# A fused retention, expert and channel-mix kernel: another spread of the weight-narrowing steps and another order inside the last routing step

## The chip, the cores and the metric

One core of one Trainium2 chip runs the whole program in one launch. The metric is the device time in microseconds (us) of that core, median of the runs; lower is better. Engine names in the rows: PE is the matrix engine (TensorE), PEld its weight loads, DVE VectorE, ACT ScalarE, POOL GpSimd, SP SyncE, which here only issues transfers.

## The reference

Three layers, one after the other, over 2 sequences of 768 tokens with 512 channels:

```python
# 1. retention over 8 heads of 64 channels, in blocks with a decayed state
intra = (q @ k^T * Dmask) @ v ;  inter = (q * lam_pow) @ kv_state ;  x = intra + inter
# 2. eight experts, one per token; a token may keep the expert of the token before it
logits = x @ w_gate ; local = sigmoid(x @ w_local)
e[s] = argmax(logits[s]) if s == 0 or local[s] < 0.5 else e[s-1]
x[s] = softmax(logits[s])[e] * (relu(x[s] @ w1[e]) @ w2[e])          # w1 512x1024, w2 1024x512
# 3. channel mix
xk = mu_k*x + (1-mu_k)*x_prev ;  xr = mu_r*x + (1-mu_r)*x_prev
out = sigmoid(xr @ w_r) * (relu(xk @ w_k)**2 @ w_v)
```

The inputs `w_k`, `w_v` and `w_r` are 64-bit floats; the kernel reads their words and turns them into 32-bit numbers itself.

## The kernel before, in words

**Split products.** Each product of two matrices runs as three (`split3`, L652): each factor is a high part, made by a cast on ACT, and a low part, made by a subtraction on DVE. For the expert weights this is `w_split` (L144): one piece of 128x1024 numbers (512 KB) is cast on ACT (L155, `w1h` or `w2h`), subtracted on DVE (L156, `w1l` or `w2l`), and then the next piece's load is queued on SP (`w_load`, L136). Four pieces (`raw`, pool `stp`) can be staged; a load waits until DVE has read the piece that had its buffer.

**First stage, to about 80 us.** Retention over 12 tiles of 128 tokens (u = 0 to 11). Then the tokens are routed, two tiles at a time, by `route` (L476), a generator whose parts are woven between the tiles' work by `step()`. The last routing (tiles 10 and 11) has nothing behind it to hide under: `logits` (L346) of both tiles, a transpose and a running maximum (`sc`), the expert of each token and its one-hot row (`ohs`, L497), counts of tokens per expert on PE (L500 to L510, into `pr` and `tot`), and from these the permutation `perm` (L516) that puts the last tiles' rows into expert 0's block. The other rows of expert 0 are gathered early (`early_rows`, L382) and transposed on PE (`first_inputs`, L435); the last rows are added to the same accumulators through `perm` (`last_inputs`, L449), with their high and low parts `xlh` and `xll`. Then a branch on the largest count (`overflow`, L388) follows, and the slots of all tokens (`slot`).

**Expert stage, about 80 to 286 us.** For e = 0 to 7: `up` (L659, four blocks `ps_h` of 24 products; ACT makes `hh`, DVE makes `hl` of each block; three accumulators, so the fourth block of `up` waits until the first block's `hh` and `hl` have been made), `flip` (L642, transposes of the next expert's gathered rows), `down` (L699, `ps_y`, two halves). After each block of `up` and twice in each half of `down`, the function `side_w` (L932) is called: 8 calls c per expert, 64 in all. A call splits one weight piece (more in the first calls) and advances the narrowing of the channel-mix weights by `ns` steps. All engines work through their instructions in the order of the program text, so what a call puts on ACT or DVE stands ahead of the next block's `hh` and `hl`.

**Narrowing** (`narrow`, L754) turns 64-bit words into 32-bit numbers, 20 parts of 128x512. A part is three steps on DVE: `narrow_1` (L743, L744), `narrow_2` (L747, L748), `narrow_3` (L751, L752). At the end of a part's third step, ACT takes the magnitudes of the next part (`begin`, L739, tile `t1`), the read of the part after the next is queued on SP (L767, 512 KB into one of two buffers `raw64`), and in the following call the finished part is written to memory (L788, 256 KB, tile `t2`). 61 steps in all; which call does how many stands in `side_w`. In expert 1 a block `weights` (L807) of small DVE and ACT work follows `flip`.

**Last stage, to the end.** The channel mix in six groups of 256 tokens, with the narrowed weights split like the experts' (the last 9 of 73 pieces).

## Time and profile before

| | us |
|---|---|
| time before, median of 3 runs | 474.19 |
| the 3 runs | 473.14 to 475.46 |
| the profiled execution's own time | 471.66 |
| its span (first to last instruction) | 470.0 |
| PE busy | 441.2 (94%) |
| DVE busy | 311.1 (66%) |
| ACT busy | 229.2 (49%) |

The profile is one execution. A row of a timeline gives start, length, engine, line, operation, output<-input, and in brackets the time that the engine stood idle before it and who released it. A row of a table of stretches gives, for each engine, its busy time in the stretch, then the granted clock of PE (1.00 is 2.4 GHz, 0.50 is 1.2 GHz), the busy share of the transfer engines and their rate. Durations of PE overlap with the next product's; the distance between starts is what counts.

### The profile page before, as it was taken

Reading aid. Unit: us, or ns where it says so; the run is one execution under the profiler, and the core shown is the slowest. Engines: PE = TensorE matmul, PEld = TensorE weight load, DVE = VectorE, ACT = ScalarE, POOL = GpSimd, SP = SyncE. Lnnn points to the kernel's source line nnn. Section 1 sums busy time; section 2 is a strip of 40 time slices with the busy share of each in tenths; the row PEclk is TensorE's granted clock in tenths of the full one; section 3 lists DMA queues with packets and bytes.
Section 4 is the critical chain, followed back from the end, with each engine's and each line's share of the span. In section 5 each row is a group of like instructions: output and inputs, shape, how many; then the busy total and the mean of one; then the engine's idle time right before and its main releaser. Section 6 shows DMA issues by size and latency. Waiting matters only on the chain.

```text
span 470.0 us, 8309 instructions
## 1 busy us (share of the span) xinstructions
PE 441.2 (94%) x3243; PEld 394.1 (84%) x3243; DVE 311.1 (66%) x602; ACT 229.2 (49%) x386; POOL 67.2 (14%) x92
## 2 busy tenths in 40 slices
PE   7999988997595799999999999999999999999996
PEld 6878876977585689898989899989898998989886
DVE  6578775767887898999998775655436253361501
ACT  2455523553663456565656463676446264563410
POOL 3432223501201103142300200100000000000000
PEclk9999999999799799999999999999999999999999
DMA  7899944697768889999988640300202002000011
GB/s 240 301 377 326 376 180 135 215 329 250 248 246 276 262 267 339 306 342 354 355 296 300 209 155 22 113 2 1 91 1 67 24 0 91 0 24 23 1 45 46
DMA packets 29111, 85.03 MB, mean 181 GB/s; under 512 B 4351, under 2 KB 5131, under 8 KB 29068
## 3 DMA queue, kind: packets, MB, share of 16 engines
q1 hardware_dynamic: 25004, 73.45, 46.2%
q0 software_dynamic: 2624, 8.39, 4.9%
q10 hardware_dynamic: 1440, 2.62, 1.5%
q8 instruction: 26, 0.43, 0.3%
q14 instruction: 17, 0.14, 0.1%
HBM read 68.71 MB, written 15.74 MB: 180 GB/s over the span
## 4 chain that ended last, share of the span: by engine, by line
PE 62%; DVE 8%; DMA 7%; ACT 4%; issue 1%; SPq 0%; DVEq 0%; ACTq 0%
PE ps_y L657 5%; PE ps_y L655 5%; PE ps_y L656 5%; PE ps_v L655 5%; PE ps_v L656 5%; PE ps_v L657 5%; PE ps_h L655 5%; PE ps_h L656 4%; PE ps_h L657 4%; PE ps_k L1028 4%; PE ps_k L1029 4%; PE ps_k L1035 4%; DMA raw<-in_wk_dram 3%; DMA wk<-t 3%; PE ps_r L656 2%; PE ps_r L655 2%
## 5 line engine op out<-in xcount | busy, mean ns | idle before, releaser
L655 PE MATMUL ps_h<-xsTh,w1h 128*128 128x256 f32 x256 | 74.4, 291 | 16.4 <-DVE hl L670 16.4
L656 PE MATMUL ps_h<-xsTl,w1h 128*128 128x256 f32 x256 | 74.0, 289 | 0.1
L657 PE MATMUL ps_h<-xsTh,w1l 128*128 128x256 f32 x256 | 73.6, 287 | 0.0
L655 PEld LDWEIGHTS ps_h<-xsTh,w1h 128*128 128x128 f32 x256 | 50.3, 197 | 17.6 <-DVE hl L670 16.8
L1067 DVE TENSOR_TENSOR sq<-rl 128x512 f32<-128x512 f32 x24 | 16.6, 691 | 55.9 <-ACT rl L1064 55.9
L655 PE MATMUL ps_y<-w2h,hh 128*128 128x512 f32 (+1 forms) x136 | 52.6, 387 | 0.0
L657 PE MATMUL ps_y<-w2h,hl 128*128 128x512 f32 (+1 forms) x136 | 52.1, 383 | 0.0
L656 PE MATMUL ps_y<-w2l,hh 128*128 128x512 f32 (+1 forms) x136 | 51.9, 382 | 0.0
L656 PEld LDWEIGHTS ps_h<-xsTl,w1h 128*128 128x128 f32 x256 | 50.3, 197 | 0.9 <-DVE xsTl L174 0.5
L657 PEld LDWEIGHTS ps_h<-xsTh,w1l 128*128 128x128 f32 x256 | 50.2, 196 | 0.0
L156 DVE TENSOR_TENSOR w1l<-raw,w1h 128x1024 fp32r<-128x1024 f32 x38 | 46.0, 1216 | 6.3 <-ACT w1h L155 6.3
L156 DVE TENSOR_TENSOR w2l<-raw,w2h 128x1024 fp32r<-128x1024 f32 x35 | 42.7, 1220 | 5.8 <-ACT w2h L155 5.2
L155 ACT CAST w1h<-raw 128x1024 fp32r<-128x1024 f32 x38 | 38.9, 1052 | 4.9 <-DMA raw<-in_w_dram 4.9
L726 POOL DMA_INDIRECT Y_n<-y,sidx x16 | 18.5, 1157 | 153.2 <-ACT y L716 108.4
L655 PE MATMUL ps_v<-w2h,k2h 128*128 128x512 f32 (+1 forms) x104 | 39.2, 377 | 0.0
L656 PE MATMUL ps_v<-w2l,k2h 128*128 128x512 f32 (+1 forms) x104 | 38.8, 373 | 0.0
L657 PE MATMUL ps_v<-w2h,k2l 128*128 128x512 f32 (+1 forms) x104 | 38.8, 373 | 0.0
L155 ACT CAST w2h<-raw 128x1024 fp32r<-128x1024 f32 x35 | 36.6, 1045 | 3.7 <-DMA raw<-in_w_dram 3.7
L739 ACT ACTIVATE t<-raw 128x512 f32<-128x512 f32 x20 | 13.5, 673 | 48.7 <-DMA raw<-in_wk_dram 24.8
L669 ACT ACTIVATE hh<-ps_h 128x512 fp32r<-128x512 f32 x32 | 19.1, 596 | 24.9 <-PE ps_h L657 24.9
L657 PEld LDWEIGHTS ps_y<-w2h,hl 128*128 128x128 f32 x136 | 25.6, 188 | 6.1 <-DVE hl L670 0.8
L656 PEld LDWEIGHTS ps_y<-w2l,hh 128*128 128x128 f32 x136 | 25.6, 188 | 5.1
(210 smaller groups left out, 975.7 us busy)
## 6 DMA issues: line engine op xcount, KB each, us to landing
raw<-in_w_dram SPq DMA_DIRECT2D x64, 512.0 KB
kv<-in_kv_dram SPq DMA_DIRECT2D x12, 512.0 KB
qk<-in_qk_dram SPq DMA_DIRECT2D x11, 512.0 KB
raw<-in_wk_dram SPq DMA_DIRECT2D x8, 512.0 KB
raw<-in_wv_dram SPq DMA_DIRECT2D x8, 512.0 KB
out_dram<-o SPq DMA_DIRECT2D x11, 256.0 KB
X_n<-xn ACTq DMA_DIRECT2D x10, 256.0 KB
xg<-Y_n SPq DMA_DIRECT2D x10, 256.0 KB
```

The source lines that it names most:

```text
L155: act.copy(out=hi[:, j : j + m, :], in_=t)
L156: eng.tensor_tensor(out=lo[:, j : j + m, :], in0=t, in1=hi[:, j : j + m, :].bitcast(F32), op=ALU.subtract)
L655: pe.matmul(ps, wh, xh, start=first, stop=False)
L656: pe.matmul(ps, wh, xl, start=False, stop=False)
L657: pe.matmul(ps, wl, xh, start=False, stop=last)
L669: act.activation(out=hh, in_=ps, func=AF.Relu)
L726: pool.indirect_dma_start(out=Y_n[:, :], out_offset=bass.IndirectOffsetOnAxis(ap=sidx[:, t, e : e + 1], axis=0), in_=y, in_offset=None)
L739: act.activation(out=t.bitcast(F32), in_=words(raw)[2], func=AF.Abs)
L1028: pe.matmul(ps[:, j, :], wkh[:, d, f], x[0][:, d, :], start=j == d == 0, stop=False, skip_group_check=True)
L1029: pe.matmul(ps[:, j, :], wkl[:, d, f], x[0][:, d, :], start=False, stop=False, skip_group_check=True)
L1035: pe.matmul(ps[:, j, :], wkh[:, d, f], x[1][:, d, :], start=False, stop=d == ND - 1, skip_group_check=True)
L1067: dve.tensor_tensor(out=sq, in0=rl, in1=rl, op=ALU.mult)
```

## The change

Five edits:

1. The steps per call (`side_w`). Before: call 2 does one step, calls 4 to 23 do 30 (two in ten of them), calls 24 to 51 one each, call 52 two. After: call 2 does one, calls 4 to 51 one each, and two where c % 8 == 5; calls 52, 53 and 54 do two each. 61 steps in both.
2. The tile `t2` gets three buffers in place of two.
3. In the last routing, the transposes `first_inputs` move from before the counts on PE to behind them; the four idle products (`warm(4)`) that stood there go, and three such products (`warm(3)`) stand where the transposes were.
4. One weight split moves from before `values` of the last tile to behind it, ahead of `logits` of tile 11.
5. The low part of tile 10's rows (`xll`, first half) is made on DVE beside that of tile 11, in place of POOL.

```diff
--- before.py
+++ after.py
@@ -374,7 +374,6 @@
             act.copy(out=hi[:, 0, :], in_=pt[:, 0])
             act.copy(out=xn[NU - B], in_=pt[:, 0])
             act.copy(out=hi[:, 1, :], in_=pt[:, 1])
-            pool.tensor_tensor(out=lo[:, 0, :], in0=xn[NU - B], in1=hi[:, 0, :].bitcast(F32), op=ALU.subtract)
             act.copy(out=xn[NU - 1], in_=pt[:, 1])
             for u in range(NU - B, NU):
                 sp.dma_start(out=X_n[1 + u * P : 1 + (u + 1) * P, :], in_=xn[u])
@@ -508,7 +507,8 @@
                 pe.matmul(tot, ones, acc, start=True, stop=False)
                 for b in range(B):
                     pe.matmul(tot, ones, oh[:, b, :], start=False, stop=b == B - 1)
-                warm(4, "pk")
+                first_inputs(0)
+                first_inputs(1)
                 oh0 = ap.tile([P, B], F32, name="oh0", bufs=1)
                 dve.tensor_copy(oh0, oh[:, :, 0])
                 perm = ap.tile([P, B, CAP], F32R, name="perm0", tag="kd", bufs=1)
@@ -518,7 +518,8 @@
                     )
                 late["perm"] = perm
                 hi, lo = late["x"]
-                dve.tensor_tensor(out=lo[:, 1, :], in0=late["nat"][:, 1], in1=hi[:, 1, :].bitcast(F32), op=ALU.subtract)
+                for b in range(B):
+                    dve.tensor_tensor(out=lo[:, b, :], in0=late["nat"][:, b], in1=hi[:, b, :].bitcast(F32), op=ALU.subtract)
                 for x in (hi, lo):
                     last_inputs(x, (0, 1))
                 for b in range(B):
@@ -606,8 +607,8 @@
                 load_kv(i + 3)
             if i == NU:
                 early_rows()
+                values(i - 1, {1: lambda: logits(i - 2)})
                 w_split()
-                values(i - 1, {1: lambda: logits(i - 2)})
                 logits(i - 1)
                 routing.append(route((i - 2) // B))
         step()
@@ -616,8 +617,7 @@
         step()
         warm(3, "pk")
         step()
-        first_inputs(0)
-        first_inputs(1)
+        warm(3, "pk")
         step()
         step()
         w_split()
@@ -776,7 +776,7 @@
             yield
             begin(0)
             for k in range(len(parts)):
-                t2 = tp.tile([P, n], I32, name="t2", tag="t2")
+                t2 = tp.tile([P, n], I32, name="t2", tag="t2", bufs=3)
                 narrow_1(ts[k])
                 yield
                 narrow_2(raws[k], ts[k], t2, ts[k])
@@ -888,7 +888,7 @@
 
         def mix_pair(i, a, hi, lo, old, new, quick=False):
 
-            t, m = (tp.tile([P, 2, 2 * P], F32, name=x, tag=x) for x in ("t1", "t2"))
+            t, m = (tp.tile([P, 2, 2 * P], F32, name=x, tag=x, bufs=k) for x, k in (("t1", 2), ("t2", 3)))
             r = slice(2 * a, 2 * a + 2)
 
             def older(j):
@@ -937,10 +937,10 @@
             ws, ns, vs = 1, 1, 0
             if c < 4:
                 ws, ns = (2, 2, 1, 1)[c], c == 2
-            elif c < 24:
-                ns = 2 if c % 8 in (4, 6) or c in (5, 7, 13, 15) else 1
             elif c >= 52:
-                ws, ns, vs = ((1, 2, 0), (1, 0, 0), (1, 0, 0), (1, 0, 0), (1, 0, 0), (1, 0, 1), (1, 0, 0), (0, 0, 1), (1, 0, 0), (1, 0, 0), (0, 0, 0), (0, 0, 0))[c - 52]
+                ws, ns, vs = ((1, 2, 0), (1, 2, 0), (1, 2, 0), (1, 0, 0), (1, 0, 0), (1, 0, 1), (1, 0, 0), (0, 0, 1), (1, 0, 0), (1, 0, 0), (0, 0, 0), (0, 0, 0))[c - 52]
+            elif c % 8 == 5:
+                ns = 2
             w_split(ws)
             for _ in range(ns):
                 next(conv, None)
```

ACT around calls 5 to 8 (the second half of expert 0's `down` and the first block of expert 1's `up`); `t<-raw` is the magnitude of a narrowing part (L739), raw_0, raw_1, raw_2 being the parts' reads, `y` a finished half of `down`, `hh` the first block of `up`. Before:

```order
L155 CAST w1h_1566<-raw_1462 128x1024
L739 ACTIVATE t_1597<-raw_1_1499 128x512
L716 COPY y_0_1604<-ps_y_0_1553 128x512
L155 CAST w1h_1566<-raw_1495 128x1024
L739 ACTIVATE t_1628<-raw_2_1599 128x512
L155 CAST w1h_1566<-raw_1532 128x1024
L716 COPY y_1_1655<-ps_y_1_1606 128x512
L669 ACTIVATE hh_0_1682<-ps_h_0_1657 128x512
L155 CAST w2h_1686<-raw_1570 128x1024
```

After:

```order
L155 CAST w1h_1565<-raw_1461 128x1024
L739 ACTIVATE t_1596<-raw_1_1498 128x512
L716 COPY y_0_1600<-ps_y_0_1552 128x512
L155 CAST w1h_1565<-raw_1494 128x1024
L155 CAST w1h_1565<-raw_1531 128x1024
L716 COPY y_1_1642<-ps_y_1_1602 128x512
L669 ACTIVATE hh_0_1669<-ps_h_0_1644 128x512
L155 CAST w2h_1673<-raw_1569 128x1024
L739 ACTIVATE t_1681<-raw_2_1598 128x512
```

The magnitude of the part raw_2 moved from ahead of a weight cast, `y_1` and `hh_0` to behind `hh_0` and one more cast.

DVE up to the first `hl` of expert 1's `up`. Before, from call 5's last instruction (the L744 of the part raw_1) on:

```order
L744 TENSOR_SCALAR t_1597<-t_1597 128x512
L156 TENSOR_TENSOR w1l_1567<-raw_1495,w1h_1566 128x1024
L747 SCALAR_TENSOR_TENSOR t_1601<-raw_1_1499,t_1597 128x512
L748 TENSOR_SCALAR t_1597<-t_1601 128x512
L751 SCALAR_TENSOR_TENSOR t_1597<-raw_1_1499,t_1597 128x512
L752 TENSOR_TENSOR t_1601<-t_1597,t_1601 128x512
L156 TENSOR_TENSOR w1l_1567<-raw_1532,w1h_1566 128x1024
L743 TENSOR_SCALAR t_1628<-t_1628 128x512
L744 TENSOR_SCALAR t_1628<-t_1628 128x512
L747 SCALAR_TENSOR_TENSOR t_1649<-raw_2_1599,t_1628 128x512
L748 TENSOR_SCALAR t_1628<-t_1649 128x512
L670 SCALAR_TENSOR_TENSOR hl_0_1683<-ps_h_0_1657,hh_0_1682 128x512
```

After, from call 5 on:

```order
L156 TENSOR_TENSOR w1l_1566<-raw_1461,w1h_1565 128x1024
L747 SCALAR_TENSOR_TENSOR t_1573<-raw_0_1496,t_1571 128x512
L748 TENSOR_SCALAR t_1571<-t_1573 128x512
L751 SCALAR_TENSOR_TENSOR t_1571<-raw_0_1496,t_1571 128x512
L752 TENSOR_TENSOR t_1573<-t_1571,t_1573 128x512
L156 TENSOR_TENSOR w1l_1566<-raw_1494,w1h_1565 128x1024
L743 TENSOR_SCALAR t_1596<-t_1596 128x512
L744 TENSOR_SCALAR t_1596<-t_1596 128x512
L156 TENSOR_TENSOR w1l_1566<-raw_1531,w1h_1565 128x1024
L747 SCALAR_TENSOR_TENSOR t_1620<-raw_1_1498,t_1596 128x512
L748 TENSOR_SCALAR t_1596<-t_1620 128x512
L670 SCALAR_TENSOR_TENSOR hl_0_1670<-ps_h_0_1644,hh_0_1669 128x512
```

Before, `hl_0` stands behind the first two steps of the part raw_2, whose L747 writes the buffer (`t_1649`) that the write of the part raw_0 to memory has to leave first; after, `hl_0` stands behind the second step of the part raw_1, and raw_2 has not begun.

The last routing on DVE: `e` is the index of the early gather, `pl` the logits of tile 10 and then of tile 11, `w2l` the weight split. Before:

```order
L385 CAST e_1086<-slot 128x2
L156 TENSOR_TENSOR w2l_831<-raw_659,w2h_830 128x1024
L355 TENSOR_REDUCE mx<-pl_1106 128x1
L356 COPY lg<-pl_1106 128x9
L357 SCALAR_TENSOR_TENSOR t_l<-lg,mx,idr 128x8
L358 TENSOR_SCALAR nk_l<-lg 128x1
L359 TENSOR_REDUCE val_l<-t_l 128x1
L360 SCALAR_TENSOR_TENSOR val_l<-val_l,pcode,nk_l 128x1
L355 TENSOR_REDUCE mx<-pl_1130 128x1
L356 COPY lg<-pl_1130 128x9
```

After:

```order
L384 CAST e_1086<-slot 128x2
L355 TENSOR_REDUCE mx<-pl_1102 128x1
L356 COPY lg<-pl_1102 128x9
L357 SCALAR_TENSOR_TENSOR t_l<-lg,mx,idr 128x8
L358 TENSOR_SCALAR nk_l<-lg 128x1
L359 TENSOR_REDUCE val_l<-t_l 128x1
L360 SCALAR_TENSOR_TENSOR val_l<-val_l,pcode,nk_l 128x1
L156 TENSOR_TENSOR w2l_831<-raw_659,w2h_830 128x1024
L355 TENSOR_REDUCE mx<-pl_1130 128x1
L356 COPY lg<-pl_1130 128x9
```

The weight split moved from ahead of tile 10's logits to ahead of tile 11's.

The same place on PE, from the transpose of the running maximum on (LDWEIGHTS rows and repeated idle products left out): `ps_x<-ident` are the transposes of the gathered rows, `pr<-ohs` and `tot` the counts, `pw` an idle product. Before:

```order
L493 MATMUL pr_1172<-ident,sc_1166 128x2
L445 MATMUL ps_x_0_1178<-ident,xs_1088 128x128 x4
L445 MATMUL ps_x_1_1183<-ident,xs_1088 128x128 x4
L500 MATMUL pr_1172<-ohs,tri 128x16
L501 MATMUL pr_1172<-acc,ones 128x16
L502 MATMUL pr_1172<-ohs,ones 128x8
L508 MATMUL tot<-acc,ones 128x8
```

After:

```order
L492 MATMUL pr_1171<-ident,sc_1165 128x2
L562 MATMUL pw<-const-bfloat16-1.0,ones 128x256
L499 MATMUL pr_1171<-ohs,tri 128x16
L500 MATMUL pr_1171<-acc,ones 128x16
L501 MATMUL pr_1171<-ohs,ones 128x8
L507 MATMUL tot<-acc,ones 128x8
L509 MATMUL tot<-ohs,ones 128x8
L509 MATMUL tot<-ohs,ones 128x8
L444 MATMUL ps_x_0_1190<-ident,xs_1088 128x128 x4
L444 MATMUL ps_x_1_1195<-ident,xs_1088 128x128 x4
```

The counts moved ahead of the transposes.

## Rows read from the trace of the kernel before

**Rows 1.** The page's first part: busy time, share of the span, instructions.

```profile
PE 441.2 (94%) x3243; PEld 394.1 (84%) x3243; DVE 311.1 (66%) x602; ACT 229.2 (49%) x386; POOL 67.2 (14%) x92
```

**Rows 2.** Stretches from one expert's transposes to the next expert's; columns in the first line.

```profile
core 0: us, PE busy (x) PEld busy (x) DVE busy (x) ACT busy (x) POOL busy (x), PEclk, DMA share, GB/s
93.67:126.86 33.19, 25.27 (x152) 22.59 (x152) 23.91 (x35) 16.70 (x23) 4.76 (x4) 0.90 0.84 280
126.86:160.87 34.01, 25.50 (x156) 23.13 (x155) 27.20 (x47) 15.97 (x23) 4.58 (x4) 0.90 0.78 260
208.57:232.13 23.56, 23.56 (x154) 21.39 (x153) 22.21 (x31) 13.86 (x19) 8.57 (x7) 1.00 0.99 353
232.13:255.70 23.57, 23.57 (x155) 21.40 (x153) 21.28 (x32) 13.88 (x19) 2.11 (x2) 1.00 0.89 315
```

**Rows 3.** Waits, 112 to 140 us: who waited for whom, total, times, longest.

```profile
ACT t L739 <- DMA raw<-in_wk_dram: 11.0, 3, 7.0
...
PE ps_h L655 <- DVE hl L670: 7.9, 1, 7.9
```

**Rows 4.** Waits, 140 to 170 us.

```profile
PE ps_h L655 <- DVE hl L670: 8.5, 1, 8.5
```

**Rows 5.** Timeline of ACT, 116 to 133 us.

```profile
116.41 0.66 ACT L739 ACTIVATE t<-raw 128x512 f32<-128x512 f32 x1 [6.95 <-DMA raw<-in_wk_dram]
...
118.38 0.60 ACT L669 ACTIVATE hh<-ps_h 128x512 fp32r<-128x512 f32 x1
...
132.31 0.67 ACT L739 ACTIVATE t<-raw 128x512 f32<-128x512 f32 x1 [3.66 <-DMA raw<-in_wk_dram]
```

**Rows 6.** Timeline of SP: two reads of narrowing parts being issued.

```profile
110.38 0.33 SPq L767 DMA_DIRECT2D raw<-in_wk_dram  x1
...
124.32 0.33 SPq L767 DMA_DIRECT2D raw<-in_wk_dram  x1
```

**Rows 7.** Timeline of DVE, 106 to 139 us.

```profile
106.54 0.43 DVE L743 TENSOR_SCALAR t<-t 128x512 f32<-128x512 f32 x1 [3.80 <-ACT t L739]
...
107.46 0.69 DVE L747 SCALAR_TENSOR_TENSOR t<-raw,t 128x512 int32<-128x512 int32 x1
...
108.54 1.22 DVE L156 TENSOR_TENSOR w1l<-raw,w1h 128x1024 fp32r<-128x1024 f32 x1
...
109.67 0.68 DVE L751 SCALAR_TENSOR_TENSOR t<-raw,t 128x512 f32<-128x512 uint32 x1
...
111.00 0.42 DVE L743 TENSOR_SCALAR t<-t 128x512 f32<-128x512 f32 x1
...
121.87 0.68 DVE L670 SCALAR_TENSOR_TENSOR hl<-ps_h,hh 128x512 fp32r<-128x512 f32 x1
...
133.49 1.29 DVE L174 TENSOR_TENSOR xsTl<-ps_x,xsTh 128x512 fp32r<-128x512 f32 x2
...
134.69 0.25 DVE L811 TENSOR_TENSOR ex<-lg,mx 128x96 f32<-128x96 f32 x1
...
138.07 1.22 DVE L156 TENSOR_TENSOR w1l<-raw,w1h 128x1024 fp32r<-128x1024 f32 x1
```

**Rows 8.** Stretches again, columns as in rows 2: first tiles, last routing, behind a wait.

```profile
8.00:10.00 2.00, 1.20 (x18) 1.00 (x17) 1.32 (x3) 0.00 (x0) 0.45 (x1) 0.87 1.03 278
74.00:76.00 2.00, 0.67 (x5) 0.44 (x5) 1.55 (x3) 1.31 (x3) 1.59 (x3) 1.00 0.60 231
122.60:125.80 3.20, 3.19 (x16) 3.19 (x17) 3.17 (x5) 1.02 (x2) 0.19 (x1) 0.54 0.94 339
```

**Rows 9.** Timeline of DVE in the last routing.

```profile
71.98 0.17 DVE L355 TENSOR_REDUCE mx<-pl 128x1 f32<-128x8 f32 x1 [1.21 <-PE pl L350]
...
74.48 1.21 DVE L513 CAST oh<-ohs 128x2 f32<-128x2 bf16 x1
...
76.89 0.74 DVE L516 TENSOR_SCALAR perm<-iotc,pr,oh 128x256 fp32r<-128x256 f16 x2 [1.19 <-PE tot L510]
```

**Rows 10.** Timeline of ACT in the last routing: both copies of tile 11's result.

```profile
70.42 0.86 ACT L314 COPY xT<-po 128x256 f32<-128x256 f32 x2 [1.95 <-PE po L310]
```

## The prediction, made before the changed kernel ran

> **What bounds the kernel now.** I read the page first: PE is busy for 94% of the span [rows 1], so only time in which PE stands still, or runs at its lower clock, can be won. Then a table of stretches, cut where each expert's transposes begin [rows 2]. The reader is to see four experts with the same work: the later two take 23.56 and 23.57 us with PE busy throughout, the first two 33.19 and 34.01, with PE busy for about 25 us and a mean granted clock of 0.90. These two stretches hold 33.19 + 34.01 - 2 x 23.57 = 20.06 us too much. The table of waits says where: once in each, PE waits for DVE's `hl`, 7.9 us [rows 3] and 8.5 us [rows 4]; and the same table shows ACT's magnitude (L739) waiting for its read, 11.0 us in three waits, one of 7.0. The rest is the clock: behind the first wait, PE works for 3.20 us at a mean granted clock of 0.54 [rows 8], which loses 3.20 x 0.46 = 1.5 us; two such make 2.9, and 16.4 + 2.9 is 19.3 of the 20.06.
>
> The timelines give the cause. SP issues the read of the third part at 110.38 [rows 6], as soon as the first part has left its buffer; it lands 6.03 us later, at 116.41, when the magnitude starts after 6.95 us of waiting [rows 5]. Behind it in ACT's queue stand a weight cast, a copy and expert 1's first `hh`, which comes at 118.38 [rows 5], and DVE's `hl` only at 121.87 [rows 7]. PE has used up its three accumulators by then. Its wait ended with that `hl` at 121.87 + 0.68 = 122.55, so it began at 122.55 - 7.9 = 114.65.
>
> **The change part by part: narrowing.** In the new order ACT has `hh_0` ahead of the third part's magnitude, so that read no longer holds `hl_0`. What is late next is DVE itself. Its unit costs are distances between starts [rows 7]: a first step 107.46 - 106.54 = 0.92, a second 108.54 - 107.46 = 1.08, a weight subtraction 109.67 - 108.54 = 1.13, a third step 111.00 - 109.67 = 1.33, a whole part 3.33; an `hl` 0.68. Up to call 4's first step, which ends at 107.46, nothing changes: the first part's read still holds ACT, and DVE idles 3.80 us for it [rows 7]. From there the new queue up to `hl_0` is split, second, third, split, first, split, second, `hl`: 3 x 1.13 + 2 x 1.08 + 1.33 + 0.92 + 0.68 = 8.48, so it ends at 115.94. PE could go on at 114.65: 1.29 us of the 7.9 stay.
>
> The next expert: from `hl_0` to the next `hl_0` DVE has 8 splits (9.04), 9 steps (9.99), 4 `hl` (2.72), two `xsTl` (134.69 - 133.49 = 1.20) and the block `weights` (138.07 - 134.69 = 3.38) [rows 7]: 26.33 us against PE's 23.57. So 2.76 us of waiting stay in place of 8.5. Without `weights`, which is there once, DVE needs 22.95 and gains 0.62 per expert on PE; I forecast no wait from expert 3 on. That is close: moving steps from calls 4 to 23 into the later ones takes experts 3 to 6 to 9 steps each in place of 8 (one step in each call before), one step of 3.33 / 3 = 1.11 more. The late steps in calls 53 and 54 lie beside expert 6's and 7's products, where no narrowing stood; the channel mix's weights are loaded behind them.
>
> The waits left, 1.29 and 2.76, I price without a slow clock. In the last routing PE was busy for only 0.67 of 2.00 us and the granted clock stayed 1.00 [rows 8].
>
> The third buffer of `t2` costs nothing and hardly matters: with a part in about three calls the write has 8.8 us (3/8 of 23.57) for what a second buffer allows already. The read is tighter. The third part's read is now issued at 107.46 + 1.13 + 1.08 + 1.33 = 111.00, lands at 117.03 if it takes 6.03 again, and the magnitude (0.66) and `hh_1` (0.60) [rows 5] end at 118.29; DVE wants `hh_1` at 115.94 + 1.13 + 1.33 = 118.40. It just fits.
>
> Narrowing gives 20.06 - 1.29 - 2.76 = 16.0 us; at best 20.06.
>
> **The last routing.** The split does not leave the path, it moves to its second half. Its cast now follows both copies of tile 11, so it starts at 70.42 + 0.86 = 71.28 [rows 10]; taken as long as the subtraction (both pass 1024 numbers), cast and subtraction end at 73.54, and tile 11's maximum, which began at 71.98 [rows 9], begins 1.56 later. From there to the one-hot cast it is 74.48 - 71.98 = 2.50 us [rows 9], so that cast falls at 76.04. `perm` began at 76.89 after waiting 1.19 for the counts [rows 9], which stood behind transposes of gathered rows. With the counts ahead, `perm` needs the cast (one of that kind should take the 0.17 of the maximum's row, not 1.21) and the counts: about 76.4, an estimate, 0.5 earlier. Behind it DVE has one subtraction more, priced like `hl`, 0.68, before the largest count and the branch. Net 0.2 later. Bounds: 0.7 earlier (`perm` right at 76.2, the subtraction hidden), 2.2 later (1.56 + 0.68, if nothing waits less). The transposes on PE now stand beside DVE's `perm` and cost nothing as long as `perm` takes its 0.74. The piece whose load moves with the split is not used before the expert stage.
>
> **Sum.** 16.0 - 0.2 = 15.8. The profiled execution took 471.66 us of its own (span 470.0): it would take 455.9. The runs' median is 2.5 higher, 474.19, and I take the difference from it: 458.4.
>
> **The rivals.**
>
> *Nothing is left of both waits*: DVE finds slack that I don't see. All 20.06 go: 454.3 with the routing's 0.2. For it: in the stretches of rows 2 with one step per call PE never waits. Against it: the queue sum. Chance 0.14.
>
> *The transfer engines become the bound.* The two long stretches moved 280 x 33.19 + 260 x 34.01 = 18.1 MB [rows 2]. Calls 4 to 19 hold 18 steps instead of 24, two parts of 0.79 MB less: 16.6 MB in 2 x 23.57 + 4.05 = 51.2 us, 323 GB/s. A later expert got 353, but at a share of 0.99 [rows 2], so the room is under a tenth. If only 280 GB/s come as in the first stretch, the 16.6 MB take 59.1 us, 7.9 more: 466.3. Chance 0.12.
>
> *The clock falls at each short wait.* The page shows it once: between 8 and 10 us, PE busy for 1.20 of 2.00 us, in pieces, had a mean grant of 0.87 already [rows 8]; against it stands the routing's 1.00. If each of seven experts had one such spell of 1.5 us, that is 10.5: 468.9. The Trainium skill (TensorE: Matmul & The Clock Gate, section "HAM oscillation") has this rule: a kernel whose blocks of products alternate with waits for data loses the clock anew in each block; by it both waits that I leave would be dearer too. The trace bears out either. Chance 0.06.
>
> *Slower: the reads come later than the queue allows.* The magnitude now has almost no margin: 118.29 against 118.40. The longest of the eight reads between 110 and 180 us took 132.31 - 124.32 = 7.99 [rows 5, 6]. At 1.86 us late (7.99 - 6.13) in each of the 18 further parts, ACT holds casts and `hh` 33.5 us in all, less DVE's spare of 0.62 in six experts (3.7): 29.8 lost against 15.8 won: 488.2. It decides from a read of about 7.2 us on (18 x (1.09 - 0.21) = 15.8). Against it: with one step per call from call 24 on, PE waited nowhere [rows 2]. Chance 0.06; a milder form, with reads near 7 us, ends within the bound of no change: 0.06.
>
> **How the numbers follow.** Forecast 458.4, chance 0.56, own range 456 to 462 (routing bounds, one or two spells of 1.5 us at the lower clock). A difference under 0.5%, 2.4 us, is no change here. The range for 8 in 10 takes in the full gain and the transfer case: 453.8 to 468. Faster: 0.56 + 0.14 + 0.12 + 0.06 = 0.88; same 0.06; slower 0.06.
>
> **What would show it.** The stretches of experts 1 and 2, cut at the transposes, should be about 25 and 26.5 us; PE's wait for `hl` near 1.3 and 2.8 us in place of 7.9 and 8.5; ACT's wait for the third part's read should stand behind `hh_0`; no lower clock between 110 and 160; the later experts still 23.6. The start of expert 0's `up` should move by less than 1 us, with the counts ahead of the transposes and tile 11's maximum near 73.5. It is wrong if an expert after the second takes over 24.5 us, if DVE idles for casts whose ACT waits for a read, or if the transfer share sits at 1.0 while PE waits.

## The result and the profile after

The changed kernel takes 460.06 us (median of 4 runs, 457.92 to 462.07), the kernel before 474.28 beside it (4 runs, 473.14 to 475.46): ratio 0.9699, 95% interval 0.9645 to 0.9754. Forecast were 458.4, range 453.8 to 468. The profiled execution took 458.98 us of its own, 12.68 less than that of before (span 457.3 against 470.0).

PE does the same work in a shorter span [rows 1]:

```profile
PE 438.2 (96%) x3242; PEld 392.7 (86%) x3242; DVE 309.7 (68%) x603; ACT 229.2 (50%) x386; POOL 65.0 (14%) x91
```

Where it went: the stretches between two experts' transposes, with the columns of [rows 2].

```profile
94.90:121.00 26.10, 24.13 (x155) 21.76 (x156) 19.66 (x27) 15.76 (x23) 5.16 (x4) 1.00 0.83 282
121.00:148.54 27.54, 25.12 (x153) 22.67 (x151) 24.76 (x42) 15.50 (x22) 4.72 (x4) 0.94 0.84 284
148.54:172.12 23.58, 23.58 (x155) 21.39 (x153) 21.59 (x31) 13.69 (x19) 3.68 (x3) 1.00 0.91 312
219.37:242.93 23.56, 23.56 (x154) 21.39 (x153) 21.43 (x32) 13.62 (x19) 1.99 (x2) 1.00 0.93 323
```

33.19 and 34.01 us became 26.10 and 27.54; the later experts stayed at 23.6. The two stretches give 7.09 + 6.47 = 13.6 us; the first one began 1.23 later than before (94.90 for 93.67). The timeline of PE has its three waits of over a microsecond there, first for expert 1's gathered rows, then for `hl` [rows 3, 4]:

```profile
94.90 0.99 PE L649 MATMUL ps_x<-ident,xs 128*128 128x128 f32 x7 [1.64 <-DMA xs<-X_n,gidx]
...
117.66 0.38 PE L655 MATMUL ps_h<-xsTh,w1h 128*128 128x256 f32 x1 [1.97 <-DVE hl L670]
...
143.92 0.58 PE L655 MATMUL ps_h<-xsTh,w1h 128*128 128x256 f32 x1 [2.42 <-DVE hl L670]
```

The timeline of ACT (beside [rows 5]) shows the order that the forecast asked for: `hh_0` at 112.38 stands ahead of the third part's magnitude. It also shows that the first part's magnitude, released by its read, began only at 107.45, and that the cast `xsTh` of expert 2's rows stands behind a magnitude that waited 4.30 us for its read:

```profile
107.45 0.67 ACT L739 ACTIVATE t<-raw 128x512 f32<-128x512 f32 x1 [6.19 <-DMA raw<-in_wk_dram]
...
112.38 0.61 ACT L669 ACTIVATE hh<-ps_h 128x512 fp32r<-128x512 f32 x1
...
116.98 0.67 ACT L739 ACTIVATE t<-raw 128x512 f32<-128x512 f32 x1 [3.06 <-DMA raw<-in_wk_dram]
117.56 0.58 ACT L669 ACTIVATE hh<-ps_h 128x512 fp32r<-128x512 f32 x1
...
127.64 0.68 ACT L739 ACTIVATE t<-raw 128x512 f32<-128x512 f32 x1 [4.30 <-DMA raw<-in_wk_dram]
128.22 1.07 ACT L173 CAST xsTh<-ps_x 128x512 fp32r<-128x512 f32 x2
```

DVE's timeline (beside [rows 7]): the first step, then `hl_0` of experts 1 and 2, between them `xsTl` of expert 2's rows with its wait for `xsTh`, and the block `weights` with its wait for ACT.

```profile
108.16 0.43 DVE L743 TENSOR_SCALAR t<-t 128x512 f32<-128x512 f32 x1 [5.19 <-ACT t L739]
...
116.93 0.68 DVE L670 SCALAR_TENSOR_TENSOR hl<-ps_h,hh 128x512 fp32r<-128x512 f32 x1
...
128.83 1.29 DVE L174 TENSOR_TENSOR xsTl<-ps_x,xsTh 128x512 fp32r<-128x512 f32 x2 [0.38 <-ACT xsTh L173]
...
132.18 0.25 DVE L814 TENSOR_REDUCE sm<-ex 128x12 f32<-128x96 f32 x1 [1.89 <-ACT sm L813]
...
143.18 0.68 DVE L670 SCALAR_TENSOR_TENSOR hl<-ps_h,hh 128x512 fp32r<-128x512 f32 x1
```

The granted clock behind PE's second wait for `hl` (columns of [rows 2]) fell to 0.50, 1.2 GHz; behind the first it stayed at 1.00:

```profile
116.00:118.00 2.00, 0.34 (x2) 0.34 (x3) 1.97 (x4) 1.02 (x2) 1.15 (x2) 1.00 0.97 327
118.00:120.00 2.00, 2.00 (x19) 2.00 (x18) 1.97 (x4) 1.66 (x4) 1.70 (x2) 1.00 0.92 294
...
142.00:144.00 2.00, 0.08 (x1) 0.09 (x1) 1.97 (x5) 0.00 (x0) 0.51 (x1) 0.98 0.99 378
144.00:146.00 2.00, 2.00 (x9) 2.00 (x10) 1.97 (x3) 1.61 (x3) 1.55 (x2) 0.50 1.05 361
146.00:148.00 2.00, 2.00 (x13) 2.00 (x13) 2.00 (x4) 1.93 (x3) 1.00 (x1) 0.67 0.84 253
```

In the last routing (DVE, then PE; beside [rows 9]) tile 11's maximum comes 1.35 later, the one-hot cast 1.35 later, `perm` 0.71 earlier. The cast takes 0.17 us in place of 1.21. PE waits 0.59 for gathered rows, and starts expert 0 at 80.20; before it was 80.31.

```profile
73.33 0.16 DVE L355 TENSOR_REDUCE mx<-pl 128x1 f32<-128x8 f32 x1
...
75.83 0.17 DVE L513 CAST oh<-ohs 128x2 f32<-128x2 bf16 x1
76.18 0.75 DVE L516 TENSOR_SCALAR perm<-iotc,pr,oh 128x256 fp32r<-128x256 f16 x2 [0.18 <-PE tot L509]
```
```profile
76.89 0.98 PE L444 MATMUL ps_x<-ident,xs 128*128 128x128 f32 x7 [0.59 <-DMA xs<-X_n,e]
...
80.20 0.35 PE L655 MATMUL ps_h<-xsTh,w1h 128*128 128x256 f32 x1
```

### The profile page after: what moved, and what is told of

Its sections match the earlier page's. It is cut to its first block, busy times and chain, and to the rows that moved or that the text cites. A ratio compares the mean times of both kernels' runs of the same rounds, so it can differ in the third digit from the quotient of the medians.

```text
span 457.3 us, 8306 instructions
## 1 busy us (share of the span) xinstructions
PE 438.2 (96%) x3242; PEld 392.7 (86%) x3242; DVE 309.7 (68%) x603; ACT 229.2 (50%) x386; POOL 65.0 (14%) x91
## 4 chain that ended last, share of the span: by engine, by line
PE 64%; DVE 8%; DMA 5%; ACT 3%; issue 2%; DVEq 0%; SPq 0%; ACTq 0%
PE ps_y L655 5%; PE ps_y L656 5%; PE ps_y L657 5%; PE ps_v L655 5%; PE ps_v L656 5%; PE ps_v L657 5%; PE ps_h L655 5%; PE ps_h L656 5%; PE ps_h L657 4%; PE ps_k L1028 4%; PE ps_k L1029 4%; PE ps_k L1035 4%; DMA raw<-in_wk_dram 4%; DVE w1l L156 2%; PE ps_r L656 2%; PE ps_r L657 2%
## 5 line engine op out<-in xcount | busy, mean ns | idle before, releaser
L739 ACT ACTIVATE t<-raw 128x512 f32<-128x512 f32 x20 | 13.6, 678 | 58.5 <-DMA raw<-in_wk_dram 25.6
L655 PEld LDWEIGHTS ps_y<-w2h,hh 128*128 128x128 f32 x136 | 25.6, 188 | 5.1
```

The source lines that it names most:

```text
L655: pe.matmul(ps, wh, xh, start=first, stop=False)
L739: act.activation(out=t.bitcast(F32), in_=words(raw)[2], func=AF.Abs)
```

## The experiments

Executions differ by up to 4 us before expert 0 starts, in kernels that are alike up to there (78.54 to 82.45). So beside the times I compare two distances inside one profile: from tile 10's maximum to the first up product (the routing), and from that product to the end of the span (the expert stage and what follows).

**Which part brings it: the schedule, the routing, the buffer, the reads.** The kernel before ran beside these four at 473.01 us.

Schedule and third buffer without the routing's edits:

```diff
-            elif c < 24:
-                ns = 2 if c % 8 in (4, 6) or c in (5, 7, 13, 15) else 1
...
+            elif c % 8 == 5:
+                ns = 2
...
+                t2 = tp.tile([P, n], I32, name="t2", tag="t2", bufs=3)
```

> The kernel before with the new schedule of steps and the third buffer, and none of the edits in the last routing. If the narrowing brings the gain, about 460 us (14 less than before, within 1.5 of the changed kernel), PE's two waits for hl near 2 and 2.5 us, the first up product at 80.3. If the last routing brings a part of it, the time lies by that part above the changed kernel's: over 2.5 us above would show it.

459.50 us, ratio 0.9725 (0.9685 to 0.9765). From the first up product (80.63) to the span's end (457.5) it took 376.9 us; the kernel before 470.0 - 80.31 = 389.7, the changed one 457.3 - 80.20 = 377.1. The narrowing is the gain. One point of the expectation missed: in expert 1 no wait for `hl` was left. PE had waited 2.08 us for the gathered rows, and behind that wait the granted clock was 0.54 and 0.60 from 96 to 100 us, which makes PE 2.00 x 0.46 + 2.00 x 0.40 = 1.7 us later still.

The routing's edits alone (old schedule, two buffers):

```diff
+                first_inputs(0)
+                first_inputs(1)
...
+                w_split()
                 logits(i - 1)
```

> The kernel before with the routing's edits alone (counts first, split and subtraction moved). If they are neutral, 474 within 1 us, first up product within 0.3 us of 80.3, waits of 7.9 and 8.5 us for hl as before. If they carry gain, over 2.4 us faster; if the 1.56 + 0.68 of added work is all on the path, 476.4.

472.69 us, ratio 1.000 (0.9973 to 1.0027): no change that can be measured. Its first up product stood at 82.97, 2.66 later than in before, but tile 10's maximum already stood 1.57 later there, and at 78 to 80 the clock was 0.50 during the routing's products. So the expected place of that product can't be tested on this execution. The other profiles bear on it: where the clock stayed at 1.00 through the routing, the distance from tile 10's maximum to the first up product was 10.49, 11.01 and 11.31 us with the old routing (before, third buffer alone, reads left out) and 10.39, 10.47 and 10.62 with the new one (changed kernel, first reads in call 1, Sigmoid moved). If the routing's edits give anything, it is about half a microsecond, which these times can't show. PE's waits for `hl` were 7.9 and 7.3 us, as good as unchanged.

The third buffer alone:

```diff
-                t2 = tp.tile([P, n], I32, name="t2", tag="t2")
+                t2 = tp.tile([P, n], I32, name="t2", tag="t2", bufs=3)
```

> The kernel before with the third buffer of t2 alone, old schedule. My theory is that the two waits for hl come from too many steps on DVE in calls 4 to 23: DVE idled for the write of an earlier part for 0.74 us ahead of the first hl and 2.26 us ahead of the second, so the third buffer gives at most 3.0 us: 471 to 473. Rival: the buffer is what mattered, 460 to 463, waits for hl near 2 us.

472.40 us, ratio 0.9992 (0.9960 to 1.0024): inside what the first theory left open, at its lower end, and far from the rival. DVE's timeline in the kernel before shows the two idle spells ahead of each late `hl`, for a cast and for a write:

```profile
118.03 1.23 DVE L156 TENSOR_TENSOR w1l<-raw,w1h 128x1024 fp32r<-128x1024 f32 x1 [2.51 <-ACT w1h L155]
...
120.80 0.69 DVE L747 SCALAR_TENSOR_TENSOR t<-raw,t 128x512 int32<-128x512 int32 x1 [0.74 <-DMA wk<-t]
...
150.12 1.22 DVE L156 TENSOR_TENSOR w1l<-raw,w1h 128x1024 fp32r<-128x1024 f32 x1 [1.93 <-ACT w1h L155]
...
154.41 0.69 DVE L747 SCALAR_TENSOR_TENSOR t<-raw,t 128x512 int32<-128x512 int32 x1 [2.26 <-DMA wk<-t]
```

With three buffers the second kind is gone, and the first grew in the second expert from 1.93 to 2.96:

```profile
150.98 1.23 DVE L156 TENSOR_TENSOR w1l<-raw,w1h 128x1024 fp32r<-128x1024 f32 x1 [2.96 <-ACT w1h L155]
```

PE's two waits sum to 14.2 us in place of 16.4, but the profile's expert stage is just 0.8 us shorter (469.7 - 80.77 = 388.9). The clock took the rest: behind the two waits PE ran 5.38 us at a mean grant of 0.66 and 7.16 at 0.61, 4.6 us lost, where in before it was 3.20 at 0.54 and 4.67 at 0.63, 3.2 us lost.

The reads of the third and later parts left out (the kernel then narrows the second part's numbers in their place, so its results are other ones):

```diff
             def read(k):
-                if k < len(parts):
+                if k > 1:
+                    raws[k] = raws[1]
+                elif k < len(parts):
```

> The kernel before, with the reads of the third and all later narrowing parts left out (those parts narrow the second part's numbers again), old schedule and buffers. By the prediction's account (the read holds ACT, and behind it hh and hl) both waits of 7.9 and 8.5 us shrink to near the 1.3 and 2.8 it leaves, and the time falls to about 460. By the rival (DVE has too many steps in its queue; it idled for casts whose ACT waited for a read only 2.51 us ahead of the first late hl and 1.93 ahead of the second) waits of about 5 and 6 us stay, and the time falls by 4 to 6, to 468 to 470.

467.81 us, ratio 0.9901 (0.9866 to 0.9936). The waits, 110 to 135 us and 135 to 165:

```profile
PE ps_h L655 <- DVE hl L670: 6.0, 1, 6.0
```
```profile
PE ps_h L655 <- DVE hl L670: 5.8, 1, 5.8
```

With no read to wait for, 6.0 and 5.8 us of the 7.9 and 8.5 remain, and the expert stage is 4.7 us shorter (467.9 - 82.92 = 385.0). So the reads made under a third of PE's waiting: 4.6 of 16.4 us, and that includes whatever the other transfers gained when these reads were gone. Of the rest, DVE's idle time for the write of a part, which stayed, is 0.93 us ahead of the first late `hl` and 2.20 ahead of the second; the remainder goes by the number of steps in DVE's queue. In expert 1, three steps less at the prediction's prices (3.33 us) would leave 5.98 - 0.93 - 3.33 = 1.7 us, close to the 1.97 of the changed kernel. The read as the main cause falls here, and the rival stands.

**What is left in the changed kernel.** Before stood at 472.09 beside the next four.

First reads in call 1:

```diff
-                ws, ns = (2, 2, 1, 1)[c], c == 2
+                ws, ns = (2, 2, 1, 1)[c], int(c == 1)
```

> The changed kernel with the narrowing's first two reads issued in call 1 in place of call 2. In the changed kernel the first part's read landed at 107.45, DVE idled 5.19 us for it, and PE waited 1.97 us for hl in expert 1 and 2.42 in expert 2, with 1.5 us at the lower clock behind the second. If the late first read is what is left, DVE's idle time shrinks by about 3 us, the wait in expert 1 goes, the one in expert 2 (DVE's 26.25 us between its hl_0 against PE's 23.57) shrinks to under 1.5, and the time falls by 2 to 4 us. Rival: the earlier reads only delay the weight reads and the gathered rows behind them; time within 1 us of the changed kernel, PE's wait for the gathered rows over 2 us.

456.14 us, ratio 0.9662 (0.9633 to 0.9692). DVE idles 1.98 in place of 5.19 for the first part, and the wait in expert 1 is gone. The one in expert 2 did not shrink, it grew: `hl_0` to `hl_0` took 139.86 - 112.45 = 27.41 us. DVE arrives early at `xsTl` of expert 2's rows and waits 1.53 us there for ACT's `xsTh`. PE had begun the transposes that it casts at 116.46, all eight within 1.03 us; ACT came to it at 124.91, because the next part's magnitude stands ahead of it and waited 5.88 us for a read. So DVE's lead is lost to a read again, at another place. DVE, ACT, then PE:

```profile
103.72 0.43 DVE L743 TENSOR_SCALAR t<-t 128x512 f32<-128x512 f32 x1 [1.98 <-ACT t L739]
125.51 1.29 DVE L174 TENSOR_TENSOR xsTl<-ps_x,xsTh 128x512 fp32r<-128x512 f32 x2 [1.53 <-ACT xsTh L173]
```
```profile
124.34 0.66 ACT L739 ACTIVATE t<-raw 128x512 f32<-128x512 f32 x1 [5.88 <-DMA raw<-in_wk_dram]
124.91 1.06 ACT L173 CAST xsTh<-ps_x 128x512 fp32r<-128x512 f32 x2
```
```profile
140.60 0.39 PE L655 MATMUL ps_h<-xsTh,w1h 128*128 128x256 f32 x1 [3.29 <-DVE hl L670]
```

From the first up product (78.54) to the end (453.9) it took 375.4, 1.7 less than the changed kernel; the interval of the ratio overlaps the changed kernel's, so by time alone a gain over the changed kernel isn't shown.

The split out of the last routing:

```diff
-                w_split()
                 logits(i - 1)
...
-                ws, ns = (2, 2, 1, 1)[c], c == 2
+                ws, ns = (3, 2, 1, 1)[c], c == 2
```

> The changed kernel with the weight split taken out of the last routing (call 0 of expert 0 does it). By the prediction's account it delays tile 11's maximum (73.33 in the changed kernel) by 1.4 us on the path, so the first up product comes 1.3 us earlier than 80.20. Rival: the path there is now the gathered rows (the transposes waited until 76.89 for them, and the products with perm stand right behind at 77.63); then the maximum comes at 71.9 and the first up product stays within 0.3 of 80.2. The time changes by less than 1.5 us in either case, so the profile decides.

457.39 us, ratio 0.9699 (0.9668 to 0.9730). Tile 11's maximum came 2.17 us behind tile 10's (68.19) in place of 3.52, and the first up product 9.10 behind it in place of 10.39 (DVE, then PE):

```profile
70.36 0.17 DVE L355 TENSOR_REDUCE mx<-pl 128x1 f32<-128x8 f32 x1 [1.22 <-PE pl L350]
```
```profile
74.10 0.98 PE L444 MATMUL ps_x<-ident,xs 128*128 128x128 f32 x7 [0.75 <-DMA xs<-X_n,e]
...
77.29 0.36 PE L654 MATMUL ps_h<-xsTh,w1h 128*128 128x256 f32 x1
```

1.3 us, as the prediction's account has it, and outside the 10.39 to 10.62 of the other profiles with this routing at full clock: the split does lie on the path. The gathered rows moved forward with it; that wait is 0.75 us.

The block `weights` one expert later:

```diff
-            if e == 1:
+            if e == 2:
                 weights()
```

> The changed kernel with the block weights moved from expert 1 to expert 2. If the wait of 2.42 us in expert 2 is DVE's queue (3.38 us of that block against 0.62 us of slack per expert), it goes from expert 2 and stands in expert 3 with 2 to 2.8 us, the distance of DVE's hl_0 there 26.3 in place of 23.6; time within 1.5 us of the changed kernel's. Rival: the reads or the transfers make the wait; then it stays in expert 2.

456.84 us, ratio 0.9719 (0.9674 to 0.9765). The wait went with the block from expert 2 to expert 3, 2.02 us; `hl_0` to `hl_0` is 164.36 - 138.53 = 25.83 there, 23.57 one expert before:

```profile
165.10 0.38 PE L655 MATMUL ps_h<-xsTh,w1h 128*128 128x256 f32 x1 [2.02 <-DVE hl L670]
```

So the block in DVE's queue makes that wait; how much a read can add to it shows below, in the second profile of the changed kernel.

Small products while PE would wait:

```diff
             for fp in range(NF // 2):
+                if e == 2 and fp == 3:
+                    pw = psw.tile([P, 512], F32, name="pf", tag="w")
+                    for _ in range(18):
+                        pe.matmul(pw[:, 0:256], ones, nc.const_aps.tensor(1.0, [P, 256], BF16), start=True, stop=True)
```

> The changed kernel with 18 small products on PE (as the warm-up ones, about 0.11 us each, 1.9 in all) just ahead of the product of expert 2 that waits 2.42 us for hl; they compute nothing that is used. If PE's standing still is what lets the granted clock fall behind that wait (0.50 between 144 and 146), it stays at 1.00, the wait left is about 0.5 us, expert 2's stretch gets 1.5 us shorter and the time falls by about that. If the clock follows something else, the stretch stays as it is. Against both: if the wait shrinks by itself, the products cost up to 1.9 us.

459.53 us, ratio 0.9743 (0.9712 to 0.9773). The median shows nothing, but the profile shows the mechanism: the products fill 2.17 us, 0.52 are left of the wait, and the clock stays at 1.00 (columns of [rows 2]):

```profile
140.08 2.17 PE L666 MATMUL pf<-const-bfloat16-1.0,ones 128*128 128x256 bf16 x18
142.77 0.39 PE L655 MATMUL ps_h<-xsTh,w1h 128*128 128x256 f32 x1 [0.52 <-DVE hl L674]
```
```profile
144.00:146.00 2.00, 2.00 (x19) 2.00 (x19) 1.97 (x4) 2.00 (x5) 1.70 (x2) 1.00 0.90 334
```

First up product to end: 455.8 - 80.45 = 375.4, 1.7 less than the changed kernel, which is what the lower clock cost there (2.00 x 0.50 + 2.00 x 0.33). With the wait filled the clock did not fall: PE's standing still is what let it fall here.

**Buffers, table load, and all together.** Before stood at 472.68 beside these.

Two buffers under the new schedule (`bufs=3` taken back in both places):

> The changed kernel with t2 on two buffers again (new schedule, new routing). If the third buffer does nothing under the new schedule, as the prediction put it, the time is that of the changed kernel, 458 to 460, and DVE shows no wait for the write of a part over 0.5 us. Rival: the write needs longer than the room that two buffers leave, DVE waits for it in most parts, and the time is over 2.4 us longer.

457.27 us, ratio 0.9690 (0.9662 to 0.9718), no wait of DVE for a write: by what these runs can tell, the third buffer moves the time in neither schedule.

The Sigmoid moved to expert 3:

```diff
-            act.activation(out=sm[:, 0], in_=ex[:, :, 0], func=AF.Sigmoid)
...
         def weights_by_slot():
+            sg = bp.tile([P, NU], F32, name="sg", bufs=1)
+            act.activation(out=sg, in_=pe_p, func=AF.Sigmoid)
```

> The changed kernel with ACT's Sigmoid of the block weights (its result is overwritten at once; ahead of it stands a table load of 1.28 us, and DVE waits 1.89 us for it) moved to expert 3, into a tile of its own. If the wait in expert 2 is DVE's queue, the distance from hl_0 to hl_0 falls from 26.25 by 1.3 to 1.9 us, and PE's wait of 2.42 to 0.5 to 1.1, with the clock at 1.00 behind it; the time falls by 1.5 to 3 us. Rival: the casts behind the table load bound DVE anyway, or the load costs the same in expert 3; time within 1 us of the changed kernel.

458.09 us, ratio 0.9665 (0.9620 to 0.9710). By time the rival stands: that is within 1 us of the changed kernel beside it (458.72). In the profile DVE's wait in the block fell from 1.89 to 0.35 and PE's to 1.56, over the 0.5 to 1.1 expected, with no lower clock behind it. `hl_0` to `hl_0` fell to 143.26 - 117.85 = 25.41, by 0.84 from the changed kernel's first profile and by 2.00 from its second (below). The two differ by DVE's wait for `xsTh`, 0.38 and 1.53 us, and 1.04 here; without it the distance fell by 1.50 from the first and 1.51 from the second, about what DVE's wait in the block lost. First up product (82.45) to end (456.9): 374.5, 2.7 less. DVE, then PE:

```profile
132.22 0.26 DVE L813 TENSOR_REDUCE sm<-ex 128x12 f32<-128x96 f32 x1 [0.35 <-ACT ex L812]
```
```profile
143.99 0.39 PE L655 MATMUL ps_h<-xsTh,w1h 128*128 128x256 f32 x1 [1.56 <-DVE hl L670]
```

Reads in call 1, split out, Sigmoid moved, and 10 small products (the edits above, together):

> Reads in call 1, the split out of the last routing, the Sigmoid in expert 3, and 10 small products ahead of the product of expert 2 that waits. If these gains are apart from one another: 2 to 3 us (reads), 1.3 (split, from tile 10's maximum to the first up product 9.1 in place of 10.4) and 1.5 to 3 (Sigmoid and clock), so 453 to 454. If they share one slack, it stays at 456.

455.28 us, ratio 0.9656 (0.9616 to 0.9696), between the two answers. In its profile PE waits over a microsecond for `hl` once, 1.04 us in expert 6, and the expert stage takes 453.6 - 78.98 = 374.6, no less than with the Sigmoid alone. That does not show that the gains share one slack: from 80 to 86 us, in expert 0, the granted clock was 0.86, 0.50 and 0.79, 1.7 us lost that the run with the Sigmoid alone did not lose (1.00 there). The question stays open. In its routing the clock stood at 0.50 from 72 to 74 us, and the first up product came 10.06 behind tile 10's maximum, not 9.1. Columns of [rows 2]:

```profile
82.00:84.00 2.00, 2.00 (x11) 2.00 (x11) 1.93 (x6) 1.67 (x2) 0.61 (x1) 0.50 0.00 0
```

It has the lowest median of all runs here, 3.4 us under the changed kernel beside it, but their intervals overlap.

The changed kernel again:

> The changed kernel unchanged, run beside the three others for the comparison: 458 to 460. Its profile shows how much its waits (1.97 and 2.42 us for hl, 1.64 for the gathered rows) and its spells at the lower clock differ from one execution to another; by the prediction's account the distance of hl_0 to hl_0 stays at 26.3 within 0.2 and the waits move with the start of the expert stage and the first read.

458.72 us, ratio 0.9714 (0.9669 to 0.9759). The distance of `hl_0` to `hl_0` is not 26.3 here but 143.33 - 115.92 = 27.41, and the waits are 1.38 and 3.57. DVE waited 1.53 us for `xsTh`, as in the run with early reads, and again behind a read: PE began the transposes at 119.63, and ACT stood 5.03 us for a read issued at 118.36 before it came to `xsTh` at 128.38. DVE, ACT, then PE:

```profile
128.98 1.29 DVE L174 TENSOR_TENSOR xsTl<-ps_x,xsTh 128x512 fp32r<-128x512 f32 x2 [1.53 <-ACT xsTh L173]
```
```profile
127.81 0.67 ACT L739 ACTIVATE t<-raw 128x512 f32<-128x512 f32 x1 [5.03 <-DMA raw<-in_wk_dram]
128.38 1.06 ACT L173 CAST xsTh<-ps_x 128x512 fp32r<-128x512 f32 x2
```
```profile
144.06 0.38 PE L655 MATMUL ps_h<-xsTh,w1h 128*128 128x256 f32 x1 [3.57 <-DVE hl L670]
```

First up product to end: 457.6 - 80.68 = 376.9, as in the first profile (377.1). DVE's `hl_0` of expert 1 came 1.01 us earlier than in the first profile (115.92 for 116.93), but the read that holds `xsTh` let ACT go on 0.17 later (127.81 for 127.64), so the lead was lost: the two waits for `hl` are 4.4 and 5.0 in sum. Taking DVE's wait for `xsTh` off, the distance is 26.25 - 0.38 = 25.87 in the first profile and 27.41 - 1.53 = 25.88 here, and 25.87 to 25.96 in the five others that keep the block in expert 1 with its Sigmoid (schedule and buffer alone, first reads in call 1, split off, small products, two buffers). So DVE's queue sets the distance, and the wait for `xsTh` adds 0 to 1.53 us to it; where it was longest, ACT had waited for a read.

## Why the prediction came out right, step by step

*The cause was half wrong.* The prediction put the late `hl` down to the read that holds ACT. With the reads of the third and later parts left out, 6.0 and 5.8 us of the waits stay. Ahead of `hl_0` DVE went from 106.54 to 121.87, 15.33 us, in before, and from 108.16 to 116.93, 8.77 us, after. The 6.56 less are its idle time of 2.51 + 0.74 and three steps less (8 became 5), 3.31 us. The sum came out all the same, because it counted DVE's queue entry by entry and left out the idle time with it. So the forecast time coming out is no evidence for the read as the cause; for the cause it was luck that the queue, and not the read, had been priced.

*Expert 1's wait, forecast 1.29, was 1.97.* The queue was right: 8.48 us to the end of `hl_0` from the end of the first step (109.10 here), and 116.93 + 0.68 - 109.10 = 8.51. What failed is "Up to call 4's first step, which ends at 107.46, nothing changes": the magnitude that waits for the read began at 107.45 in place of 105.84. The first two reads were issued at 99.44, and at 99.16 in before, so it is the read itself that took 8.01 us in place of 6.68. PE lost part of that by itself, at the gathered rows (1.64 for 0.31), so the wait grew by just 0.68. In the seven other profiles with this schedule and the first reads in call 2 it was 0.93 to 1.82 us in six and nothing in one, so the forecast lies among what single executions show.

*Expert 2's wait, forecast 2.76, was 2.42 and 3.57.* The distance between `hl_0`s, forecast 26.33, was 26.25 and 27.41. The first is nearly right by two errors against each other, and PE's own way from the first wait to the second was 23.84 us, not 23.57 (117.66 to 143.92 - 2.42). The queue alone took 25.87 and 25.88, 0.45 less than the sum: 0.32 of that is the four `hl`, priced at their length of 0.68, where the next instruction starts 0.60 behind (116.93 to 117.53). And the sum has no term for DVE's waiting for `xsTh`, 0.38 and 1.53 us, behind a magnitude that waits for its read. This is the prediction's own sign of being wrong, "if DVE idles for casts whose ACT waits for a read", and the mechanism of its slower rival. The sum checked the third part's read against `hh_1`, which it did not delay, and not the next part's read against `xsTh`, which it did.

*"The waits left, 1.29 and 2.76, I price without a slow clock" failed at the second wait.* 144 to 146 at 0.50 and 146 to 148 at 0.67 lose 1.7 us. The small products show that the standing still caused it. For its rival "the clock falls at each short wait" the prediction cited the Trainium skill (TensorE: Matmul & The Clock Gate, section "HAM oscillation"), by which each block of products behind a wait for data starts at the lower clock. That section of the Trainium skill tells this of a kernel that waits about 3 to 5 us between its blocks; the waits that the prediction applied it to were forecast at 1.29 and 2.76. The trace agrees at the second wait, 2.42 us, and with `weights` later at 2.02, and not at the first, 1.97. Seven spells, as that rival had it, did not come, for want of waits: from expert 3 to the end of expert 7 PE never stood for `hl`.

*The later experts* were right: 23.56 to 23.68 us and no wait. Their steps were not: by the edit, expert 6 does ten (calls 48 to 55) where it did six, and not nine in place of eight, and calls 53 and 54 lie in expert 6; PE did not wait there either. The slower rival (reads beyond DVE's queue) came in expert 2 alone as far as PE's waits go, by 0.38 and 1.53 us: behind expert 3's transposes DVE waited 1.53 us for `xsTh` too, and PE did not wait. The transfer bound did not come: the first stretch moved 282 GB/s, as little as in before, in 26.10 us in place of 33.19, and PE waited for `hl`, not for weights.

*The last routing* was forecast 0.2 later and began expert 0 0.1 earlier; the run with its edits alone shows no change. Maximum 73.54 (73.33 measured), one-hot cast 76.04 (75.83), its time 0.17 (0.17), `perm` 76.4 (76.18): each within 0.22. Taking the split out gave 1.3 us there in the one profile taken, so its place on the path is shown.

*The third buffer* costs and brings nothing that can be measured in the time, in either schedule.

*The sum.* 15.8 forecast; the profiles give 12.7, the medians 14.2, and 14.0 when both kernels ran again (472.68 - 458.72). The terms that were off in the first profile: the first stretch began 1.03 later than forecast (94.90 for 93.67 + 0.2), as the wait for the gathered rows, for which the sum has no term, was 1.64 for 0.31; then 0.68 in expert 1's wait, 1.7 for the clock, and 0.34 the other way in expert 2's wait: 15.8 - 1.03 - 0.68 - 1.7 + 0.34 = 12.7. Why the gathered rows came later stays open; over the fourteen profiles that wait was 0.31 to 2.08 us in thirteen and nothing in one.

## What to carry to other kernels

Count the queue of the in-order engine between two of its results that PE needs, entry by entry; the longest wait in a table of waits may be covered by that queue, and is then not what its removal brings. Spread side work evenly over the calls, and look for what a block that comes once (here `weights`, with a table load in ACT) adds to one period. A lead of the helper engine is lost at the next transfer that it waits for, itself or through another engine's queue, so filling an earlier gap can enlarge a later wait. Check each read against everything that stands behind it in its reader's queue, and not only against the entry that was late before.

## What the runs showed of the hardware

The granted clock falls at different places in executions of one program. Kernels that are alike up to expert 0 started it between 78.54 and 82.45. In the changed kernel's first profile the clock stood at 0.50 from 8 to 14 us, in the run with early reads at 1.00 there; in the changed kernel's second profile it was 1.00 from 8 to 12 and 0.50 from 74 to 78, in the routing. A difference of under 2 us between two single profiles of this kernel is therefore read from distances within a stage, and the clock of that stage has to be looked at too, as the run with all edits together shows (0.50 from 82 to 84 us).

From 90 us on, in the profiles with the new schedule, the clock fell (to 0.50 to 0.55 in the lowest stretch of 2 us) behind PE's waits of 2.02, 2.08, 2.13, 2.33, 2.42, 2.54, 3.29 and 3.57 us and nowhere else; behind those of 1.97 and less it stayed at 1.00. That of 2.08 was for gathered rows, the others for `hl`.

Reads of a part (128 x 512 numbers of 8 bytes) take very different times: in the changed kernel the first, issued at 99.44, was there at 107.45, the third, issued at 112.14, at 116.98. That is 8.01 and 4.84 us; the first took 6.68 in before, and the fourth, issued at 118.36 and there at 127.81, 9.45 in the changed kernel's second profile. The three waits of DVE for `xsTh` that took 1.53 us (there, with early reads, and ahead of expert 3 in the first profile) have one thing more in common: ACT went on 1.05 or 1.06 us after SP had issued the next read (127.81 for 126.75, 124.34 for 123.28, 155.06 for 154.01). What ties the two, no run shows.

```profile
99.44 0.80 SPq L767 DMA_DIRECT2D raw<-in_wk_dram  x2
...
112.14 0.33 SPq L767 DMA_DIRECT2D raw<-in_wk_dram  x1
```
